# Products with v in four 64x64 pieces of TensorE, and one load of weights issued behind the next output product

## The chip, the cores and the metric

The kernel runs on one core of one Trainium2 chip. Its time is device time in microseconds. The median of the three runs shown is 1360.17 us (1358.74 to 1366.19).

TensorE is called PE here, VectorE DVE, ScalarE ACT, GpSimd POOL, SyncE SP. SP issues nearly all DMA transfers, in order, from one queue.

## The reference

An attention with a threshold is followed by a gated feed-forward block, all in float32.

```python
# q, k, v: (8, 8, 576, 64), tau: 0.02
scores = scale * np.matmul(q, k.transpose(0, 1, 3, 2))
thresh = np.max(scores, axis=-1, keepdims=True) - tau
scores = np.where(scores >= thresh, scores, -1000000000.0)
attn = np.exp(scores - np.max(scores, axis=-1, keepdims=True))
attn = attn / (np.sum(attn, axis=-1, keepdims=True) + 1e-09)
attn_out = np.matmul(attn, v)
# (batch, head, seq, dim) -> (batch * seq, head * dim) = (4608, 512)
x = attn_out.transpose(0, 2, 1, 3).reshape(4608, 512)
g = x @ w_gate                       # (512, 1536)
silu = g * (1.0 / (1.0 + np.exp(-g)))
out = (silu * (x @ w_val)) @ w_out   # (1536, 512)
```

## The kernel before, in words

**Order of the work.** Batch 0 is handled first, in a way of its own (up to about 143 us in the trace), and isn't touched. The other seven batches have four segments each, one for each pair of heads: 28 segments. A segment has three slots. In a slot PE computes the scores of three times 64 queries of two heads against all 576 keys (`slot_scores`, L1849, matmul at L1865), and DVE, ACT and POOL turn them into weights of the attention (`slot_rest`, L1870): maxima (L1886, L1888), exponential (L1911), mask with sum (L1913), scaling (L1936, L1939), transposition in blocks of 32 (L1941). A block of twelve slots belongs to one batch; `kk` counts them from 0 to 11.

In the second slot of each segment but the first (`x == 1`, so `kk` 1, 4, 7, 10) the main loop first calls `attend` for the segment before (L1946), and straight after it `slot_scores` of this slot. The last segment is attended behind the loop (L2168), where output products follow.

**The products with v.** `attend` multiplies the weights of the attention by v for two heads of 64 columns and 576 queries. The keys are spread over the 128 partitions in two halves `a` of 64 rows and, in each, nine steps `j`. Half `a` adds up in a PSUM bank of its own, `holds[a]`, over the nine steps. The innermost loop (`x`, L1960) cuts the 128 output rows (two heads of 64 columns of v) into four parts of 32: `h` is the head and `ds` the half of v's columns. So a product has 64 rows of v by 32 columns as weights, 288 columns of the attention's weights pass by it, and 2 halves by 4 parts make eight pieces of PE's array. An attend has 9 x 2 x 4 = 72 such products. In the profile a float32 product shows as two MATMUL records, each with a LDWEIGHTS record of its own: 28 x 72 x 2 = 4032 records at L1962. The scores use pieces of the same 64x32 shape (L1865, 32 products a slot).

**What fills the slots.** Between the scores of one slot and the next, PE works on the feed-forward block of the batch before: the products with w_gate and w_val in six groups `g` (`Group`, L1035, steps p1, p5, p2, p6, p3, p7, p4; matmul at L1052), then the products with w_out. Both are computed with seven products of sums in place of eight (a Strassen scheme), the latter nested once more in the batches from `DEEP` (2) on (`Deep`, L1527; matmul at L1598). How many steps stand in which slot is written out in tables (`GV`, `CD`, L2064 to L2073).

For these batches `Deep`'s steps stand in the order p1, gates_end, p2, p7, p6, p4, p5, p3 (L1547). By `CD` p1 and gates_end come in slot 9, two steps each in slots 10 and 11, p5 in slot 0 of the next block and p3 in slot 1, where it stands behind that slot's attend and scores. Two steps of the next gates, p1 and p5 of group 0, follow in the same slot 1. In the last block p5 stands ahead of the attend behind the loop, p3 behind it.

**The loads of weights.** In the batches from `DEEP` on, the weights of a group and their sums come anew from HBM, in seven parts in the ring `flow` of two places (`load_flow`, L982; DMA at L985): parts 0 to 3 (1024 KB) and parts 4 to 6 (768 KB), the "later weights". Group `g` uses place `g % 2`. `Deep` uses the same room for its sums, so the loads of the first two groups for the next batch are issued from `Deep`'s steps when the room comes free: `self.next_flow(g, part, m)` (L1838) makes a job for SP that depends on the product `m`. Group 1's later weights go where the sums for p5's product lay (`flow_end`, written from p7). p3 of group 1 reads them first; in the last batch DVE makes sums from them first (`deepen_weights`, L1195).

**What sets the order.** A planner (`Plan`, L28) walks through PE's work in the order of the program. Every job of another engine has an engine, a duration, dependencies and a rank; SP's also have a time to landing. The planner emits the jobs of each engine in the order in which they would start. So a changed dependency can change the order of the jobs in the queues of SP, DVE, ACT and POOL. PE's order is that of the program. An attend counts 4.5 us in the plan (L1965).

Of the kernel before, what the change touches and what calls it, by code (L numbers as in the profile page):

```python
# [27 lines left out]
class Plan:  # L28
# [12 lines left out]
    def job(self, eng, took, fn, *deps, rank=1, lag=0.0, moves=0.0):  # L41
        j = Job(eng, took, fn, rank, lag, moves)
        for d in deps:
            if isinstance(d, Job) and d.end is None:
                d.then.append(j)
                j.waits += 1
            elif d is not None:
                j.ready = max(j.ready, self.after(d, eng) if isinstance(d, Job) else d + self.HOP)
        if not j.waits:
            self.open[eng].append(j)  # L50
        return j
# [45 lines left out]
    def pe(self, took, fn, *deps):  # L97
        self.force(*deps)
        for d in deps:
            if d is not None:  # L100
                self.t = max(self.t, (d.end if isinstance(d, Job) else d) + self.HOP)
        self.run(self.t)
        fn()
        self.t += took
        return self.t + self.PIPE
# [39 lines left out]
def kernel(  # L145
# [11 lines left out]
    nc = tc.nc  # L157
# [6 lines left out]
    G = 32  # L164
    NG = P // G
# [3 lines left out]
    NK = NJ // 2  # L169
    SM = 512  # L170
    NT = SM // P
    SH = S // 2
# [278 lines left out]
    heads = [slice(h * D, (h + 1) * D) for h in range(2)]  # L451
# [104 lines left out]
    def attend_tile(copy=lambda xa, fn: (fn(), give_back(xa))):  # L556
        if not unattended:
            return
        if not xts:
            for u, lo in enumerate((0, 2 * XW)):  # L560
                xts["full", u] = xall[:, lo:lo + XW].rearrange("p (c n) -> p c n", c=NCC)
            xts["last", 0] = xlast
        seg, t, pT, pT2 = unattended.popleft()
        vr, vr2 = seg["v"]
        n = pT2.shape[1]
        xa = bank("xa")
        for kt in range(KT):
            for h in range(2):
                nc.tensor.matmul(xa[h * D:(h + 1) * D, 0:n], vr[:, h, kt, :], pT[:, h, kt, :],  # L569
                                 start=(kt == 0), stop=False)  # L570
        nc.tensor.matmul(xa[:, 0:n], vr2, pT2, start=False, stop=True)
        u, lo = divmod(t * P, TC)
        to = xts[("last", 0) if t == NT else ("full", u)][:, seg["i"], lo:lo + n]
        copy(xa, lambda: nc.scalar.copy(to, xa[:, 0:n]))
# [305 lines left out]
    def take(name, full=False):  # L880
        free = [b for b in banks if (not b.held if b.fixed is not None else b.n in turns)]
        if full:
            free = [b for b in free if b.full]
            return Hold(min(free, key=Bank.free_at), name) if free else None
        n = sum(b.full for b in free)
        return Hold(min(free, key=lambda b: (b.full and n == 1, max(b.free_at(), plan.t))), name)
# [17 lines left out]
    def pool_tt(out, a, b, op):  # L904
        return lambda: nc.gpsimd.tensor_tensor(out=out, in0=a, in1=b, op=op)  # L905
# [84 lines left out]
    def x_place(c, kh):  # L990
        lo = c % 2 * XW if kh == 0 else 2 * XW
        return xall[:, lo:lo + XW].rearrange("p (t c n) -> p t c n", t=2, c=2)
# [7 lines left out]
    def token_sums(c, c2, deps, eng="POOL"):  # L1000

        x11, x12, x21, x22 = (x_block(c, t, kh)[:, c2] for t in range(2) for kh in range(2))
        s1, s2, s4 = (x[:, c2] for x in xs)
        tt, took = (pool_tt, 0.75) if eng == "POOL" else (dve_tt, 0.36)
        j1 = job(eng, took, tt(s1, x21, x22, ALU.add), *deps, rank=0)
        j2 = job(eng, took, tt(s2, s1, x11, ALU.subtract), j1, rank=0)
        j4 = job(eng, took, tt(s4, x12, s2, ALU.subtract), j2, rank=0)
        j3 = job(eng, took, tt(x21, x11, x21, ALU.subtract), j1, rank=0)
        jobs = ready_x.setdefault(c, {n: [] for n in range(5)})
        for n, j in ((1, j1), (2, j2), (3, j3), (4, j4)):  # L1010
            jobs[n].append(j)
        jobs[0] += deps
# [22 lines left out]
    class Group:  # L1035
# [32 lines left out]
        def p5(self):  # L1068
            self.take_b()
            self.e = take("pe")  # L1070
            m = self.mul(self.e, self.w[2], xs[0], True, *self.w_deps[2], *ready_x[self.c][1], *self.e.deps)
            self.e.bank.full = True
            s, old = turn_of(s_bufs)
            self.s = s
            self.s5 = job("ACT", 0.55, lambda: nc.scalar.activation(s.ap, self.e.rows(), AF.Copy, scale=0.5), m, *old, rank=0)
# [38 lines left out]
        def p3(self):  # L1114
            m = self.mul(self.e, self.w[5], xs[2], False, self.s5, *self.w_deps[5], *ready_x[self.c][4])
            u = self.u1_buf
            g1 = job("DVE", 0.7, lambda: nc.vector.scalar_tensor_tensor(out=u.ap, in0=self.e.rows(), scalar=0.5, in1=u.ap, op0=ALU.mult,
                                                                        op1=ALU.add), m, self.u1, rank=0)
            self.e.read_by(g1)
            self.e.done(True)  # L1120
            self.finish(0, u, g1, self.a, self.m2)
# [405 lines left out]
    class Deep:  # L1527
# [250 lines left out]

        def p5(self):
            m = self.nested(4, self.x, False, *self.c6)  # L1780
            self.next_flow(1, 1, m)
            t, t7 = self.spaces[0:2]
            self.c5 = self.copies(t, self.x, m, *self.z)
            n, j = self.combine(t7, job("POOL", 2.2, pool_tt(t7, t7, t, ALU.add), *self.c5, *self.c7, rank=1))
            self.ship(1, 1, n, j)
            for b in u_list:
                b.jobs = [*b.jobs, j]

        def p3(self):
            m = self.nested(2, self.x, False, *self.c5)  # L1790
            n, j = self.combine(self.x, m, psum=True)
            self.done(self.x, j)
            self.ship(0, 1, n, j)
# [152 lines left out]
    def attend(seg):  # L1946
        i = seg["i"]
        b, cc = divmod(i, NP)
        base = seg["p"]
        p = pall[:, base:base + 2 * NK * SH].rearrange("p (k h j q) -> p h k j q", h=2, j=NK, q=G)  # L1950
        vr = seg["v"]
        R, rows = 2, P // 2
        holds = [take("xa") for _ in range(R)]
        assert cc < 2 or "last_product" not in state

        def fn():
            for j in range(NK):
                for a in range(R):
                    rs = slice(a * rows, (a + 1) * rows)
                    for x in range(NG):  # L1960
                        h, ds = x // 2, slice(x % 2 * G, (x % 2 + 1) * G)
                        nc.tensor.matmul(holds[a].ap()[x * G:(x + 1) * G, 0:SH].rearrange("d (i q) -> d i q", q=G),  # L1962
                                         vr[rs, h, j, ds], p[rs, h, :, j, :], start=(j == 0), stop=(j == NK - 1))

        m = pe(4.5, fn, *seg["turned"], seg["vj"], *holds[0].deps, *holds[1].deps)  # L1965
        kh, c2 = divmod(cc, 2)
        xk = x_place(b, kh)[:, :, c2, :].rearrange("p t (i a q) -> p a t i q", a=2, q=G)
        xl = xlast[:, cc, :].rearrange("p (a q) -> p a q", a=2)
        js = x_jobs.setdefault(b, [])
        lo, at_last = 0, 2 * NT * G  # L1970
        for a in range(R):
            def copy(a=a):
                nc.scalar.copy(xk[:, a], holds[a].ap()[:, lo:lo + 2 * NT * G].rearrange("p (t i q) -> p t i q", t=2, q=G))
                nc.scalar.copy(xl[:, a], holds[a].ap()[:, at_last:at_last + G])
            js.append(job("ACT", 0.65, copy, m, last_store[0] if cc == 0 else None,
                           *(sixth_kept if b == DEEP + 1 else ()), rank=0))
            holds[a].read_by(js[-1])
            holds[a].done(False)
            holds[a].bank.full = False
        if cc == NP - 1:  # L1980
            store_last(b, *js)
        if cc >= 2:
            token_sums(b, c2, js[2 * c2:2 * c2 + 2] + js[2 * cc:] + [stores[2]], "DVE" if tail[0] else "POOL")
        return m

    def store_last(b, *deps):
        w = S - SM
        last_store[0] = job("SP", 0.1, lambda: nc.sync.dma_start(out=last_hbm[:, :, b * w:(b + 1) * w], in_=xlast), *deps, lag=3.0)
# [135 lines left out]
    for s, (n, x) in enumerate((n, x) for n in range(len(halved)) for x in range(NU3)):  # L2124
        seg = halved[n]
        i, t = seg["i"], seg["tiles"][x]
# [11 lines left out]
        elif s == 1:  # L2138
            box = []
            m = pe(1.0, lambda: attend_tile(lambda *y: box.extend(y)))  # L2140
            j = job("ACT", 0.27, box[1], m, rank=0)
# [43 lines left out]
    for c in (B - 1, B):  # L2185
# [4 lines left out]
        if c < B:  # L2190
            w = SM // 2
            j = []
# [43 lines left out]
```

## Time and profile before

| | |
|---|---|
| timed runs | 1360.17, 1358.74, 1366.19 us |
| profiled execution | 1362.1 us, of which the span from first to last instruction is 1360.2 us |
| PE's clock | 0.999 of full speed |
| PE busy | 1341.3 us (99%), 15,770 matmul records |
| DVE, ACT, POOL busy | 1072.6, 876.0, 689.1 us |
| L1962, products with v | 4032 records, 129.3 us |
| L1865, scores | 5376 records in two lengths (288 and 144 columns), 165.9 us |
| L985, loads into `flow` | 84 issues, landing after 4.2 to 9.6 us, 5.0 in the median |
| queue q8, kind "instruction" | 125 packets, 2.05 MB |

The page gives busy time by engine, then the queues of the DMA, and the chain: the work that ended last, followed back to what released it. A group's line has the source line, the engine, the operation, the target and the sources, the shapes, the count, then busy time in us and the mean of one in ns, then idle time ahead of it and what ended that. A matmul's record is longer than its share of PE's time, because matmuls overlap; what counts is the time from start to start. A line of the waits has the one who waited, the one waited for, the total in us, how often, and the longest. "issue" means that the engine waited for nothing that the profile shows. A line of the timeline has the start, the length, the engine, the line, the operation and the count of the instructions drawn together in it. SPq is SP's queue of DMA issues; its lines span from the first to the last issue that were drawn together, waits between them included.

### The profile page before, as it was taken

Reading aid. Unit: us, or ns where it says so; the run is one execution under the profiler, and the core shown is the slowest. Engines: PE = TensorE matmul, PEld = TensorE weight load, DVE = VectorE, ACT = ScalarE, POOL = GpSimd, SP = SyncE. Lnnn points to the kernel's source line nnn. Section 1 sums busy time; section 2 is a strip of 40 time slices with the busy share of each in tenths; the row PEclk is TensorE's granted clock in tenths of the full one; section 3 lists DMA queues with packets and bytes.
Section 4 is the critical chain, followed back from the end, with each engine's and each line's share of the span. In section 5 each row is a group of like instructions: output and inputs, shape, how many; then the busy total and the mean of one; then the engine's idle time right before and its main releaser. Section 6 shows DMA issues by size and latency. Waiting matters only on the chain.

```text
span 1360.2 us, 39655 instructions
## 1 busy us (share of the span) xinstructions
PE 1341.3 (99%) x15770; PEld 1115.8 (82%) x15770; DVE 1072.6 (79%) x2839; ACT 876.0 (64%) x2260; POOL 689.1 (51%) x717
## 2 busy tenths in 40 slices
PE   8999999999999999999999999999999999999998
PEld 6777777787788788878887888878887789999998
DVE  6888898878887777778787877877787776787786
ACT  6888777777756767677776766776767774330330
POOL 2588397543464669624982379426952495000000
PEclk9999999999999999999999999999999999999999
DMA  8752424555525532554164515553255405424411
GB/s 196 183 187 93 81 56 134 149 137 145 152 68 162 148 98 68 152 159 127 37 188 129 150 36 147 137 151 87 89 156 145 114 22 174 158 78 147 157 61 32
DMA packets 210760, 166.28 MB, mean 122 GB/s; under 512 B 166288, under 2 KB 182160, under 8 KB 205200
## 3 DMA queue, kind: packets, MB, share of 16 engines
q1 hardware_dynamic: 206656, 162.83, 42.2%
q8 instruction: 125, 2.05, 0.6%
q10 hardware_dynamic: 3920, 0.92, 0.4%
q14 instruction: 59, 0.48, 0.1%
HBM read 141.30 MB, written 22.41 MB: 120 GB/s over the span
## 4 chain that ended last, share of the span: by engine, by line
PE 94%; DVE 2%; POOL 1%; DMA 1%; issue 1%; ACT 0%; DVEq 0%; SPq 0%; POOLq 0%
PE pb L1052 18%; PE pa L1052 12%; PE px L1598 12%; PE sc L1865 10%; PE xa L1962 9%; PE pe L1052 9%; PE po L1331 5%; PE py L1598 3%; PE pv L1256 2%; PE pg L1256 2%; PE sc L1213 2%; PE py L1607 2%; PE sc L468 1%; PE pe L1213 1%; PE tp L538 1%; PE xa L569 1%
## 5 line engine op out<-in xcount | busy, mean ns | idle before, releaser
L1913 DVE SCALAR_TENSOR_TENSOR pall<-sc,th,pall 128x288 f32<-128x288 f32 x504 | 244.4, 513 | 58.4 <-ACT pall L1911 39.9
L1052 PE MATMUL pb<-xall,big 128*128 128x256 f32 x1152 | 273.3, 380 | 0.0
L1911 ACT ACTIVATE pall<-sc,nm 128x288 f32<-128x288 f32 x504 | 232.8, 497 | 39.0 <-DVE pall L1913 38.9
L1052 PEld LDWEIGHTS pb<-xall,big 128*128 128x128 f32 x1152 | 216.5, 190 | 30.7 <-issue 2.2
L1941 DVE STREAM_TRANSPOSE pall<-pall 128x576 f32<-128x576 f32 x252 | 188.9, 764 | 30.7 <-ACT pall L1939 22.3
L1939 ACT ACTIVATE pall<-pall,ri 128x288 f32<-128x288 f32 x413 | 189.9, 528 | 30.8 <-DVE ri L1927 30.4
L1052 PE MATMUL pa<-xall,big 128*128 128x256 f32 x768 | 183.6, 382 | 0.0
L905 POOL TENSOR_TENSOR hall<-hall,tmp 128x512 f32<-128x512 f32 x80 | 102.5, 1282 | 155.3 <-DVE hall L1105 137.1
L1886 DVE TENSOR_REDUCE mx<-sc 128x2 f32<-128x576 f32 x168 | 125.7, 748 | 52.4 <-PE sc L1865 52.2
L1052 PEld LDWEIGHTS pa<-xall,big 128*128 128x128 f32 x768 | 142.9, 190 | 22.4 <-issue 2.7
L1865 PE MATMUL sc<-kT,qT 64*32 64x288 f32 (+1 forms) x5376 | 147.1, 345 | 5.0 <-issue 3.4
L1865 PEld LDWEIGHTS sc<-kT,qT 64*32 64x32 f32 x5376 | 95.9, 106 | 57.1 <-issue 18.4
L1052 PE MATMUL pe<-xall,big 128*128 128x256 f32 x576 | 137.3, 381 | 0.0
L1962 PE MATMUL xa<-pall,vall 64*32 64x288 f32 x4032 | 129.3, 404 | 0.6 <-issue 0.6
L1052 PEld LDWEIGHTS pe<-xall,big 128*128 128x128 f32 x576 | 108.4, 190 | 17.0 <-issue 2.5
L1962 PEld LDWEIGHTS xa<-pall,vall 64*32 64x32 f32 x4032 | 74.0, 107 | 48.2 <-issue 6.8
L1936 POOL TENSOR_SCALAR pall<-pall,ri 128x288 f32<-128x288 f32 x91 | 45.2, 511 | 93.3 <-DVE ri L1927 92.9
L1921 ACT COPY sums<-sums 32x6 f32<-32x6 f32 x336 | 66.6, 198 | 36.8 <-DVE pall L1913 31.9
L905 POOL TENSOR_TENSOR tmp<-tmp 128x512 f32<-128x512 f32 (+1 forms) x41 | 56.5, 1377 | 63.7 <-ACT tmp L1127 62.2
L905 POOL TENSOR_TENSOR big<-hall 128x384 f32<-128x384 f32 (+2 forms) x69 | 65.3, 970 | 33.2 <-PE pa L1052 26.1
L1104 ACT ACTIVATE vall<-tmp 128x512 f32<-128x512 f32 x96 | 60.1, 629 | 27.8 <-POOL tmp L905 13.5
L1888 DVE TENSOR_REDUCE mx<-sc 128x1 f32<-128x288 f32 x168 | 75.0, 447 | 0.0
(279 smaller groups left out, 2503.2 us busy)
## 6 DMA issues: line engine op xcount, KB each, us to landing
big<-sums_hbm SPq DMA_DIRECT2D x42, 1024.0 KB, 5.3
big<-sums_hbm SPq DMA_DIRECT2D x48, 768.0 KB, 4.4
vall<-in_v_dram SPq DMA_DIRECT2D x112, 144.0 KB, 2.9
out_dram<-big SPq DMA_DIRECT2D x32, 256.0 KB, 2.4
qT<-in_q_dram SPq DMA_DIRECT2D x112, 72.0 KB, 4.8
kT<-in_k_dram SPq DMA_DIRECT2D x112, 72.0 KB, 2.9
wo<-in_moe_w_gate_dram SPq DMA_DIRECT2D x16, 384.0 KB, 3.5
wo<-in_moe_w_val_dram SPq DMA_DIRECT2D x16, 384.0 KB, 4.1
```

Source lines behind the costliest of these rows:

```text
L905: return lambda: nc.gpsimd.tensor_tensor(out=out, in0=a, in1=b, op=op)
L1052: nc.tensor.matmul(ps[:, i], w[:, k_, i * P:(i + 1) * P], x[:, k_, :], start=first and i == k_ == 0, stop=True, skip_group_check=True)
L1331: nc.tensor.matmul(ps, h(f), w[:, f, :], start=(f == 0), stop=(f == NF2 - 1))
L1598: nc.tensor.matmul(ps, a[:, f, :], ws[n][:, f, :], start=bank_ not in begun, stop=True, skip_group_check=True)
L1865: nc.tensor.matmul(pss[h][(slice(g * G, (g + 1) * G), *part)], qT[hs, col:col + G], kT[hs, c * SH + keys[0]:c * SH + keys[1]], start=True, ...
L1886: rs.append(job("DVE", 0.72, lambda n=n, tile_=tile_: nc.vector.tensor_reduce(out=mx[:, n:n + 2, 0], in_=tile_[:, :, 0:SH], axis=AX.X, op= ...
L1888: rs.append(job("DVE", 0.42, lambda n=n, tile_=tile_: nc.vector.tensor_reduce(out=mx[:, n + 2:n + 3, 0], in_=tile_[:, :, SH:SH + SQ], axis ...
L1911: ej = job("ACT", 0.42, lambda x=x, n=n: nc.scalar.activation(ps[x], scs[x], AF.Exp, bias=nm[:, n:n + 1]), ej, masks.get((h, u - 1)), rank=0)
L1913: masks[x] = job("DVE", 0.45, lambda x=x, n=n: nc.vector.scalar_tensor_tensor(out=ps[x], in0=scs[x], scalar=th[:, n:n + 1], in1=ps[x], op0 ...
L1939: scaled.append(job("ACT", 0.46, lambda x=x, n=n: nc.scalar.activation(x, x, AF.Copy, scale=ri[:, n:n + 1]), rj, rank=rank))
L1941: seg["turned"].append(job("DVE", 0.72, lambda both=both: nc.vector.transpose(out=both, in_=both), *scaled, rank=rank))
L1962: nc.tensor.matmul(holds[a].ap()[x * G:(x + 1) * G, 0:SH].rearrange("d (i q) -> d i q", q=G), vr[rs, h, j, ds], p[rs, h, :, j, :], start=( ...
```

## The change

Two edits. In `attend` the inner loop runs over the two heads instead of over four parts of 32 columns. A product then has 64 rows by 64 columns of weights and writes 64 partitions; 9 x 2 x 2 = 36 products in place of 72, over four pieces of the array in place of eight. Operands, banks and the planned time are the same. (`heads` is `[slice(0, 64), slice(64, 128)]`, L451.)

In `Deep`, the line that issues the load of group 1's later weights for the next batch moves from p5, where it depended on p5's product, to p3, where it depends on p3's product. p5 and p3 are the last two output products of a batch. This applies to the five batches 2 to 6; `p3_flat`, used at the end of the program, isn't changed.

```diff
         def p5(self):
             m = self.nested(4, self.x, False, *self.c6)
-            self.next_flow(1, 1, m)
             t, t7 = self.spaces[0:2]
             self.c5 = self.copies(t, self.x, m, *self.z)
             n, j = self.combine(t7, job("POOL", 2.2, pool_tt(t7, t7, t, ALU.add), *self.c5, *self.c7, rank=1))
...
         def p3(self):
             m = self.nested(2, self.x, False, *self.c5)
+            self.next_flow(1, 1, m)
             n, j = self.combine(self.x, m, psum=True)
             self.done(self.x, j)
             self.ship(0, 1, n, j)
...
                     rs = slice(a * rows, (a + 1) * rows)
-                    for x in range(NG):
-                        h, ds = x // 2, slice(x % 2 * G, (x % 2 + 1) * G)
-                        nc.tensor.matmul(holds[a].ap()[x * G:(x + 1) * G, 0:SH].rearrange("d (i q) -> d i q", q=G),
-                                         vr[rs, h, j, ds], p[rs, h, :, j, :], start=(j == 0), stop=(j == NK - 1))
+                    for h, hs in enumerate(heads):
+                        nc.tensor.matmul(holds[a].ap()[hs, 0:SH].rearrange("d (i q) -> d i q", q=G),
+                                         vr[rs, h, j, :], p[rs, h, :, j, :], start=(j == 0), stop=(j == NK - 1))
```

## The prediction, made before the changed kernel ran

> **What bounds the kernel now.** I read the page's first part, then its queues and chain, then who PE waited for.
>
> ```profile
> PE 1341.3 (99%) x15770; PEld 1115.8 (82%) x15770; DVE 1072.6 (79%) x2839; ACT 876.0 (64%) x2260; POOL 689.1 (51%) x717
> ...
> q8 instruction: 125, 2.05, 0.6%
> ...
> PE 94%; DVE 2%; POOL 1%; DMA 1%; issue 1%; ACT 0%; DVEq 0%; SPq 0%; POOLq 0%
> ```
>
> ```profile
> PE sc L468 <- DVE pall L492: 3.5, 4, 1.1
> PE sc L1865 <- issue: 3.4, 5, 1.5
> PE sc L468 <- DVE cap L704: 2.0, 1, 2.0
> PE sc L1865 <- DVE pall L1913: 1.6, 1, 1.6
> PE idle L278 <- DVE pall L260: 1.3, 1, 1.3
> PE xa L1962 <- issue: 0.6, 1, 0.6
> ```
>
> PE is the bound: 99% busy, 94% of the chain. Only two of its waits lie where the change works, and both name "issue": six stops in which PE waited for no engine and no data. All others lie before 143 us, ahead of the first product with v (171.1 us). So in the loop whatever PE time is added or saved goes straight to the end.
>
> The six stops are these. I counted PE's records (LDWEIGHTS, MATMUL, semaphore) from the start. The stops come right behind records 7616, 10432, 13504, 18368, 19392 and 25536. Each is 192 above a multiple of 256. The queue q8 moved 125 packets, 2.05 MB, so 16.4 KB each; PE has 32,084 records, 257 per packet. So each packet is a block of 256 PE instructions, and PE stops where a block ends and the next hasn't come. The packets confirm it: the six late ones ended at 339.76, 451.12, 561.20, 742.84, 782.53 and 999.71 us, and PE went on 1.3 to 1.6 us after each. Beyond the normal step the stops took 0.40, 0.49, 1.62, 0.78, 0.36 and 1.30 us, together **4.95 us**. Here is the longest, in the timeline of PE and then that of SP's queue:
>
> ```profile
> 555.20 4.59 PE L1962 MATMUL xa<-pall,vall 64*32 64x288 f32 x144
> 559.59 1.65 PE L1865 MATMUL sc<-kT,qT 64*32 64x288 f32 x58
> 562.70 0.44 PE L1865 MATMUL sc<-kT,qT 64*32 64x144 f32 x6 [1.46 <-issue]
> ```
>
> ```profile
> 555.33 0.35 SPq L985 DMA_DIRECT2D big<-sums_hbm  x1
> 559.83 2.68 SPq L441 DMA_DIRECT2D vall<-in_v_dram  x4
> ```
>
> An attend followed by scores is where records go fastest: 288 (144 matmul records and their weight loads) in 4.4 us, then 128 in 1.9 us, 15 ns each. The products over 256 columns take 2 records in 215 ns. A block is asked for about 320 records before it is needed (estimate: no packet started more than 297 records ahead; the rest is the 1 us that the quickest took to start). The tightest 320 records of the loop pass in 4.4 us; from asking to usable (landing plus 1.4 us) the loop's 103 blocks took 3.5 to 9.4 us, median 4.8. Every block whose 320 records lie in an attend and its scores is therefore at risk, and PE stops if a big load stands ahead of it.
>
> **Part 1: the products with v.**
>
> ```profile
> L1962 PE MATMUL xa<-pall,vall 64*32 64x288 f32 x4032 | 129.3, 404 | 0.6 <-issue 0.6
> L474 PE MATMUL sc<-pall 64*64 64x288 f32 x32 | 4.8, 415 | 0.0
> ...
> L1962 PEld LDWEIGHTS xa<-pall,vall 64*32 64x32 f32 x4032 | 74.0, 107 | 48.2 <-issue 6.8
> L474 PEld LDWEIGHTS sc<-pall 64*64 64x64 f32 x32 | 1.9, 132 | 2.1 <-DVE pall L492 1.0 <-issue 0.3
> ```
>
> Of 4,032 records 2,016 go, and as many weight loads: 28 attends of 72 products become 28 of 36, each product being two records.
>
> *The rounds.* Record by record, an attend is 18 rounds of 8: in a round the starts are 6.7 ns apart, and the next round starts 242.5 ns after the last (288 columns). So the 8 pieces run together, and a round costs what one product costs. With four pieces it is 18 rounds of 4. The same 4.365 us, if four 64x64 pieces run together. No row shows four: L474's round has two on the diagonal, 243 ns; L569 has two beside each other on the same rows, 109 ns a round for 128 columns. Each direction overlaps; I take four together. The other end, two by two, is a rival. Weight loads get longer, 107 to 132 ns, still under 242 ns and hidden.
>
> *The entry.* The first product waits for its weights: 427 instead of 402 ns at L1962, 453 at L474. So +26 ns, 28 times: **+0.73 us**.
>
> *The exit.* 27 of 28 attends are followed by scores of the same shape, 64x32, and their first product comes 243 ns after the first of the last round, without a break. After the change the shape differs. Every change of shape in the trace has a break: 332 ns from start to start for 288 columns (242.5 without), 309 for 256 (216), 203 for 128 (109), 212 for 144 (122); it is the same when only the columns change (L569 to L571, 203) and only the rows (L474 to L569, 332). So the scores start 20 (three steps of 6.7) + 332 ns after the first of the last round, and expose 25 ns of weight load: 377 for 243, +134 ns, 27 times: **+3.62 us**. From 64x64 to 64x32 isn't in the trace; the ends are 0 (no break) and 134, and I take 134, since both kinds of change beside it have it. The Trainium skill (TensorEngine Tiling (Array Packing), Key Properties) says that changing the tiling mode, not just the tile, drains the array; by this the exit is paid, without it the sum is the second rival's.
>
> *The stops.* With 144 records in place of 288, I took every second attend record out of the trace and looked again at all stretches of 320 records: the tightest is now 8.6 us, not 4.4. Four of the 103 blocks took that long, none beside a tightest stretch. So all six stops go: **-4.95 us**. Next late would be a block of over 8.6 us in an attend.
>
> **Part 2: the load of the second group's later weights** (L985, 768 KB, five times) moves from behind the product of p5 to that of p3. Nothing is added or removed. At 555.33 us it was issued just as an attend began; the late block was asked for at about 556.2 us and started at 560.27, when the load was landing (5.0 us in the median). The stop at 1000 us is the same picture (load 993.93, block 998.78). So this edit by itself takes away the causes of 1.62 + 1.30 us, which part 1 also covers; it isn't counted twice. On SP it is moved past an output store, the load of v and the store of the last columns, which come earlier. Its new place: p3 ends at 567.9 us; SP's queue holds two output stores there until 571.5; landing takes 4.2 to 9.6 us, so 576 to 581; first read by the third product of group 1 at 590.5 us. 9 us of cover; without it PE would wait up to that excess. In the last block DVE adds up these weights (L908, four of 0.42 us at 1150.08), read by PE at 1161.25: the load would come at about 1147.8, land at 1152 to 1157 and be summed by 1159. Cost 0; at the late end DVE holds up its queue by some 2 us (what stands behind: the quarters from 1156.57), upper end +2 us.
>
> **Sum**: -4.95 + 0.73 + 3.62 = **-0.60 us**. The profiled execution took 1362.1 us (span 1360.2), so 1361.5 for such a one. The median of the timed three is 1360.17, 1.9 lower: if they stop as long, 1359.6; if what they lack is stops (3.0 us of them), 1361.5. I take the middle: **1360.5 us**.
>
> **Rivals.**
> 1. *Slower: the break isn't repaid.* Price +4.35 us, 1364.5. It decides wherever the timed runs stop for less than 4.35 us in all. For: their stops can't be seen, and 1358.74 is 3.4 below the profiled time. Against: six stops with exact places, and timed runs that spread over 7.5 us, as late blocks would make them. The Trainium skill (Runtime: NRT & Kernel Launch, Instruction fetch mechanics) describes blocks of 256 instructions, which the trace bears out, but calls the fetch mostly hidden and gives PE room for 2,048; with that room no block would be late, and this rival would hold. The trace speaks against: blocks start at most 297 records ahead. Chance 0.20.
> 2. *Faster than forecast: no break between 64x64 and 64x32.* Only the entry is paid: 1360.17 - 4.95 + 0.73 = 1356.0. Against: all changes of shape seen have one. Chance 0.12.
> 3. *The pieces run two by two*: 18 more rounds of 242.5 ns in 28 attends, +122 us, 1482. Against: L569 and L474. Chance 0.02.
> 4. *The moved load comes late* or the planner, which now places other work around it, makes an engine late in each block: over 6.8 us in all, some 1368. Chance 0.06.
> 5. *Timed runs stop longer than the profiled one* (1366.19 is 7.4 above the lowest): 8 us or more saved, 1353 or less. Chance 0.05.
> The forecast has 0.55.
>
> **The numbers.** Within 0.5% (1353.4 to 1367.0, about what a measurement of this kernel can tell from no change): the forecast, 1 and 2, less a little at the edges, 0.82; faster 0.08 (5 and the edge of 2); slower 0.10 (3, 4, the edge of 1). Range: low end rival 2, 1355.5; high end rival 1 plus 2 us for the late load, 1366.5.
>
> **What would show it.** L1962 with 2,016 records of 64x64, 4.4 us an attend; 18 rounds of 242.5 ns with 4 starts each; first product 453 ns; scores 332 ns behind the last product; no idle of PE put down to issue between 171 and 1143 us; 109 or 110 packets on q8 (15.75 blocks fewer); L985's moved load issued at the gates' first product, and no wait of PE for it. I am wrong if the scores follow without a break, if a round lasts 485 ns, if stops remain, or if PE waits for L985.

## The result, and the profile after

The changed kernel takes **1357.59 us** in the median of 11 runs (1356.68 to 1358.54); the kernel before, beside it, 1361.26 us in 11 runs (1358.04 to 1366.19). The ratio is **0.9972** (95% interval 0.9962 to 0.9983): 3.7 us faster. 1360.5 us was forecast, no change to speak of. The time lies in the range given, but the kernel became faster, clear of the interval. The profiled execution took 1357.13 us, span 1355.3.

The page after, the same lines:

```profile
PE 1343.2 (99%) x13754; PEld 1112.5 (82%) x13754; DVE 1071.6 (79%) x2839; ACT 875.8 (65%) x2260; POOL 688.9 (51%) x717
...
q8 instruction: 109, 1.79, 0.6%
...
PE 94%; DVE 2%; POOL 1%; ACT 1%; DMA 1%; issue 0%; DVEq 0%; ACTq 0%; POOLq 0%; SPq 0%
```

PE's waits after; no line names L1865 or the products with v (L1961) any more:

```profile
PE sc L468 <- DVE pall L492: 3.0, 5, 1.1
PE sc L468 <- DVE cap L704: 1.7, 1, 1.7
...
PE xa L569 <- ACT big L545: 0.3, 1, 0.3
```

PE has 2,016 records fewer and yet 1.9 us more busy time: fewer records don't make the attends shorter. What went is a wait. The two lines with "issue" at L1865 and L1962 (3.4 and 0.6 us) are gone, and 16 packets fewer came on q8. The products with v, by form, and the stretch that held the longest stop before, on PE and on SP's queue:

```profile
L1961 PE MATMUL xa<-pall,vall 64*64 64x288 f32 x2016 | 128.7, 405 | 0.0
L1961 PEld LDWEIGHTS xa<-pall,vall 64*64 64x64 f32 x2016 | 74.4, 133 | 47.3 <-issue 5.6 <-DVE pall L1913 0.3
```

```profile
552.98 4.59 PE L1961 MATMUL xa<-pall,vall 64*64 64x288 f32 x72
557.51 1.72 PE L1865 MATMUL sc<-kT,qT 64*32 64x288 f32 x64
559.15 1.60 PE L1598 MATMUL px<-wo,hall 128*128 128x128 f32 x12
```

```profile
557.61 2.73 SPq L441 DMA_DIRECT2D vall<-in_v_dram  x4
560.42 0.57 SPq L1987 DMA_DIRECT2D last_hbm<-xlast  x1
562.59 0.41 SPq L1659 DMA_DIRECT2D out_dram<-big  x1
563.04 0.46 SPq L985 DMA_DIRECT2D big<-sums_hbm  x1
```

Half the records in the same 4.59 us; the scores run through, 64 records without a hole; the load stands 10 us after the attend's start.

To compare executions I take PE's time from the start of the third slot's scores (150 to 154 us) to its last product. It is 1200.01 us in the changed kernel, where nothing stops PE, and 1202.72 in the one before. So the change itself brings **2.7 us** in the profiles. The other 2.3 us between the two spans lie ahead of that, where the change does nothing (the second slot's scores come at 141.8 us before and at 139.5 after).

### The profile page after: what moved, and what is told of

It reads as the page before. It is cut to its first block, busy times and chain, and to the rows that moved or that the text cites. A ratio compares the mean times of both kernels' runs of the same rounds, so it can differ in the third digit from the quotient of the medians.

```text
span 1355.3 us, 35619 instructions
## 1 busy us (share of the span) xinstructions
PE 1343.2 (99%) x13754; PEld 1112.5 (82%) x13754; DVE 1071.6 (79%) x2839; ACT 875.8 (65%) x2260; POOL 688.9 (51%) x717
## 4 chain that ended last, share of the span: by engine, by line
PE 94%; DVE 2%; POOL 1%; ACT 1%; DMA 1%; issue 0%; DVEq 0%; ACTq 0%; POOLq 0%; SPq 0%
PE pb L1052 19%; PE pa L1052 13%; PE px L1598 12%; PE sc L1865 10%; PE xa L1961 9%; PE pe L1052 9%; PE po L1331 5%; PE py L1598 3%; PE pg L1256 2%; PE pv L1256 2%; PE sc L1213 2%; PE py L1607 2%; PE pe L1213 1%; PE sc L468 1%; PE pv L585 1%; PE xa L569 1%
## 5 line engine op out<-in xcount | busy, mean ns | idle before, releaser
L1865 PE MATMUL sc<-kT,qT 64*32 64x288 f32 (+1 forms) x5376 | 144.9, 346 | 0.0
L1865 PEld LDWEIGHTS sc<-kT,qT 64*32 64x32 f32 x5376 | 90.9, 106 | 58.0 <-issue 25.1
L1961 PE MATMUL xa<-pall,vall 64*64 64x288 f32 x2016 | 128.7, 405 | 0.0
L1961 PEld LDWEIGHTS xa<-pall,vall 64*64 64x64 f32 x2016 | 74.4, 133 | 47.3 <-issue 5.6
```

The costliest lines, as they stand in the source:

```text
L1865: nc.tensor.matmul(pss[h][(slice(g * G, (g + 1) * G), *part)], qT[hs, col:col + G], kT[hs, c * SH + keys[0]:c * SH + keys[1]], start=True, ...
L1961: nc.tensor.matmul(holds[a].ap()[hs, 0:SH].rearrange("d (i q) -> d i q", q=G), vr[rs, h, j, :], p[rs, h, :, j, :], start=(j == 0), stop=(j ...
```

## The experiments

The theory: PE stops where its next block of 256 instructions comes late; the change takes all stops away and pays a break at 27 exits and a longer entry. Rivals: the moved load is what helps and the four pieces only cost; the difference comes from the head of the program.

**The kernel before, once more.**

> The kernel before once more, unchanged, for a second profile. Theory A (PE stops where a block of 256 instructions comes late): stops put down to issue between 171 and 1143 us, each behind a record that is 192 above a multiple of 256, at least four of them, 4 to 9 us in all with what follows them; not all in the same places, since the DMA's moments vary. Rival C (the head of the program makes a good part of the difference): the first scores of the loop start at 130.3 us and the second at 141.8 again, as in the first profile of before, and not 0.6 and 2.3 us earlier as in the changed kernel.

1360.82 us profiled. Four stops, behind records 7616, 13504, 19392 and 25536, four of the former six places, 5.2 us of gaps beyond the normal step. A fifth, behind record 10432, is too short for a line; its slot lost 0.37 us against the same slot without a stop.

```profile
PE sc L1865 <- issue: 4.5, 4, 1.7
...
PE sc L1865 <- DVE pall L1913: 1.4, 1, 1.4
```

From the third slot on it took 1202.67 us, the first profile 1202.72. Its first two slots' scores came at 128.8 and 140.1 us, 1.5 and 1.8 us earlier than in the first profile. So the head varies by itself by nearly as much as the two spans differed there, and the loss in the loop stays. The rival that the head makes the difference falls for the 2.7 us of the loop; how much of the timed 3.7 us lies in the head isn't shown.

**Part 1 alone.** The kernel before with only this edit:

```diff
-                    for x in range(NG):
-                        h, ds = x // 2, slice(x % 2 * G, (x % 2 + 1) * G)
...
+                    for h, hs in enumerate(heads):
```

> Part 1 alone: four pieces of 64x64, the load still behind p5. Theory A: half as many records in an attend are enough; no stop put down to issue between 171 and 1143 us, 27 breaks of 332 ns, time as the changed kernel's: 0.997 of before (0.996 to 0.9985). Rival B (the load at the attend's start is the cause): stops stay at some of the five attends behind p5, 0.5 to 2 us each, and the time is 0.998 to 1.000.

1357.64 us against 1359.76, ratio 0.9982 (0.9974 to 0.9991). No stop in the loop; 1200.06 us from the third slot on, as with both edits. The load is issued right after the attend's start, as before, and nothing comes late:

```profile
553.90 4.59 PE L1961 MATMUL xa<-pall,vall 64*64 64x288 f32 x72
558.42 1.72 PE L1865 MATMUL sc<-kT,qT 64*32 64x288 f32 x64
```

```profile
554.03 0.40 SPq L985 DMA_DIRECT2D big<-sums_hbm  x1
```

So half the records are enough, and in the loop the moved load adds nothing to them. Fewer records also put the blocks' ends elsewhere, and four pieces with other ends weren't run. But five of the six late blocks of the first profile were usable 5.4 to 6.4 us after they were asked for (the sixth 9.4), and with four pieces no 320 records of the loop pass in under 8.6 us, wherever a block ends.

**Part 2 alone.** The line moved from p5 to p3, eight pieces of 64x32 kept.

> Part 2 alone: eight pieces of 64x32, the load moved behind p3. Theory A: the stops at the attends behind p5 go (3.3 of 6.5 us in the first profile), those at other attends stay, no breaks: 0.9975 (0.9965 to 0.9985), as good as the change as a whole. Rival B: nearly all stops go and 1353 to 1355 us are reached (0.995), since no breaks are paid. If the load is no cause: 1.000 and stops behind p5 as before.

1356.14 us against 1359.76, 0.9971 (0.9961 to 0.9982): by itself it does as much as the whole change. The stops behind p5 are gone (560 and 1000 us), and with the other timing that at 743 us as well; three are left:

```profile
PE sc L1865 <- issue: 1.0, 3, 0.5
```

From the third slot on 1198.39 us, 1.6 less than with four pieces: it keeps 1.5 us of gaps and pays no breaks.

**More transfers at the attends**, in the kernel before and in the changed one. Nothing reads the copy:

```diff
+            was = halved[n - 1]
+            job("SP", 0.1, lambda lo=was["p"]: nc.sync.dma_start(out=spare_hbm, in_=pall[:, lo:lo + 6 * SH]), *was["turned"], plan.t,
+                lag=2.0, moves=3.4)
             prepare_v(seg, attend(halved[n - 1]))
```

> The kernel before with one more transfer at each of 27 attends: 884 KB of the attention's weights copied to a spare place in HBM (nothing reads it), issued by SP when these weights are ready and the attend is planned. Theory A: with full transfers in the way the block comes late at most attends where one ends; some 10 or more stops, 10 to 25 us more in all, 1.007 to 1.02. Rival (stops depend on the place in the program alone and not on transfers): 1.000 to 1.002.

> The changed kernel with the same extra copy of 884 KB at 27 attends that made the kernel before 1.2% slower (10 stops, 15 us). Theory A: with half the records the delay still fits; none or two short stops, 0.997 to 1.000 of before, at most 3 us above the changed kernel. Rival (the copies cost time by something else than stops, such as late operands): 1.007 to 1.012 here too.

Before: 1376.16 us against 1359.76, 1.0122 (1.0097 to 1.0147). Ten stops, 15.7 us of gaps beyond the normal step, each at the end of a block, up to 3.4 us:

```profile
PE sc L1866 <- issue: 12.8, 8, 3.3
...
PE xa L1963 <- issue: 1.4, 2, 1.0
```

The longest, where two big transfers stand one behind the other ahead of the block:

```profile
563.16 1.65 PE L1866 MATMUL sc<-kT,qT 64*32 64x288 f32 x59
568.07 0.69 PE L1866 MATMUL sc<-kT,qT 64*32 64x144 f32 x5 [3.26 <-issue]
```

```profile
558.90 0.47 SPq L986 DMA_DIRECT2D big<-sums_hbm  x1
559.49 0.37 SPq L2131 DMA_DIRECT2D spare_hbm<-pall  x1
```

The changed kernel with the same copies: 1357.43 us against 1361.72, 0.9970 (0.9959 to 0.9982), no stop, 1200.01 us. So by themselves the transfers cost nothing, and half the records stand them.

In the kernel before, the ten stops cost more than their gaps: against slots without a stop 24.7 us. At the three longest (2.7, 3.4 and 3.2 us) the trace shows a granted clock of 0.5 for 3.4, 6.8 and 3.4 us, and their slots lost 1.9, 3.1 and 1.9 us beyond the gap; the other seven, of up to 2.2 us, left the clock at 1.0 and lost 0.2 to 0.5 us beyond it.

**Half a block further on.** In the kernel before, 128 short records at the head, while PE waits for its first data:

```diff
+    short = bank("idle")
+    for _ in range(32):
+        nc.tensor.matmul(short[0:G, 0:G], ones[0:G, 0:G], ones[0:G, 0:G], start=True, stop=True)
+    give_back(short)
```

> The kernel before with 32 short idle products (32x32 weights, 32 columns; 128 records of PE, about 2 us while PE waits for the first loads) at the head, whose result nothing reads. All later instructions lie half a block further on. Theory A (the block's end decides): stops again only behind records that are 192 above a multiple of 256, so at other places of the program: none of the places of before (340, 452, 560, 743, 783, 1000 us); instead some of those where 320 records now pass in under 5 us (near 240, 306, 376, 488, 526, 596, 635, 705, 742, 962, 1032, 1070 us), most likely 705 and 742, where a load of weights stands ahead of the attend. Two to six stops, 1 to 7 us; 0.997 to 1.002. Rival (the places are set by the transfers or by the program's steps alone): stops again near 340, 560, 783 and 1000 us.

1356.70 us against 1361.26, 0.9962 (0.9945 to 0.9980). Three stops, behind records 6848, 17600 and 27584, each 192 above a multiple of 256: near 305, 704 and 1070 us, three of the twelve places named, none of the old ones. A fourth, behind record 15552 at 633 us, also on the list (635), is too short for a line; its slot lost 0.27 us. Of the two called most likely, 705 us came and 742 did not. The ratio lies a little under the range expected, 0.997 to 1.002.

```profile
702.72 1.40 PE L1869 MATMUL sc<-kT,qT 64*32 64x288 f32 x37
705.10 0.71 PE L1869 MATMUL sc<-kT,qT 64*32 64x144 f32 x27 [0.97 <-issue]
```

```profile
698.47 0.35 SPq L989 DMA_DIRECT2D big<-sums_hbm  x1
```

32 idle products make the kernel before about as fast as the change did: from the third slot on it took 1200.04 us. The end of the block decides where PE stops.

**Holding back the other loads.** To the load behind p3, this adds: the loads that were issued just before an attend wait in a list until its scores are in the program.

```diff
+                if self.g == 1 and not tail[0]:
+                    held.append((load_flow, (self.c, self.g + 2, 0)))
+                else:
+                    load_flow(self.c, self.g + 2, 0, plan.t + plan.PIPE)
...
+                elif self.g == 3 and not tail[0]:
+                    held.append((load_flow, (self.c, self.g + 2, 1, m)))
...
         pss, mark = slot_scores(seg, t)
+        if x == 1:
+            release(mark)
```

(`release` issues the jobs in the list, with the end of the scores as a further dependency in the plan; `load_sums` of group 3 in batch 1 is held in the same way.) First with eight pieces of 64x32, then with four of 64x64:

> The kernel before with the load behind p3 and, besides, the other loads of weights that were issued just before an attend held back until its scores are planned (group 3's first parts, group 5's later parts, and in batch 1 group 3's sums); eight pieces of 64x32. Theory A: the three stops that part 2 alone left (1.5 us of gaps, 2.0 with what follows them) go, none or one stop stays, no breaks are paid: 0.9955 of before (0.9945 to 0.9965), some 2 us under part 2 alone and 3.5 to 4 under the changed kernel. Rival (stops only move to other attends): as part 2 alone, 0.997.

> The same held loads with four pieces of 64x64. With no stops on either side the difference to the run before it is what the shape costs by itself. Theory A: 27 exits and 28 entries at 0.15 us, +4.1 us: 0.9985 of before, as the changed kernel. If the breaks are hidden somewhere: as the run before it.

Eight pieces: **1353.92 us** against 1361.72, 0.9949 (0.9935 to 0.9962), the best version here. One stop is left (338 us):

```profile
PE sc L1880 <- issue: 0.5, 1, 0.5
```

Four pieces, same loads: 1357.66 us, 0.9975 (0.9965 to 0.9985), no stop, 1200.01 us from the third slot on against 1196.94. The one stop made its slot 0.86 us longer than the same slot without one. With that taken off, eight pieces need 1196.1: four pieces cost 3.9 us. That is the shape by itself.

## Why the prediction was wrong

The mechanism was right in its main parts: PE stops at late blocks, half the records take the stops away, and every change of shape costs a break. Two of its sizes and one choice were off: the stops went into the sum with 4.95 us and cost 6.6, the breaks with 4.35 and cost 3.9, and the timed runs were taken to stop less than the profiled one.

- **The stops.** Place, cause and disappearance were right. Their size wasn't: I counted the gaps, 4.95 us. Slot by slot against runs without them (the kernel with both edits for three, part 2 alone for the others), the six cost 0.64, 0.71, 1.85, 1.25, 0.60 and 1.53 us, together **6.6 us**. Behind a gap the records of the first round are longer (307 ns for 282; the 25 ns are what an exposed weight load costs at an attend's start, 427 for 402), and the rounds of eight come broken. Together that is 0.2 us for five of them and 0.5 us for the one inside an attend. The prediction's four blocks of 8.6 us or more leave one out: the late block of 742.84 us took 9.4 us, over 320 records that passed in 8.4. Its stop, too, is gone in the changed kernel.
- **The breaks.** 332 ns at each of the 27 exits and 453 ns at the entries, as worked out; four pieces run together, rounds of 242.5 ns with starts 6.7 ns apart (the first round of an attend 293 ns, for 266 before). From the scores ahead of an attend to those behind it PE took 0.137 us longer, and in the next slot 0.014, together 0.151 instead of 0.161: the exposed weight load of the scores' first product shows as 14 ns, not 25. At the first attend the next slot gave the loss back. So the breaks cost **3.9 us**, not 4.35.
- **The sum** would then have been -6.6 + 3.9 = -2.7 us, as measured, in place of -0.6. A small difference of two terms that are each seven or eight times as large moves by as much as their errors.
- **From the profile to the timed runs.** I took the profile's 1.9 us above the median of three runs as a hint that timed runs stop less, and moved the forecast up from 1359.6 to 1360.5. The runs speak against it: what they gain, plus 3.9 us of breaks, is 7.6 us in this comparison, and 6.0 to 8.2 us in the other three with a kernel whose profile shows no stop. So they lose about as much as the profile's 6.6 us, or more; how much of it lies in stops can't be seen in them. The spread points the same way: 8.2 us before, 1.9 us after. Part of it goes with the clock: of 45 runs of the kernel before beside the experiments, the 14 with a granted clock of 1.0 took 1359.1 us in the mean and the seven with 0.997 or less 1363.5. Whether the clock fell behind stops there, as it did with the added copies, isn't shown; the version with held loads and four pieces, without a stop in its profile, also has one such run (0.997, 1360.68 us).
- **Part 2** costs nothing, as said: no wait of PE for it. It was issued at 563.0 us, during p3 and not behind it: the data it overwrites are p5's, so only the planner's order holds it, not p3's end. In the last blocks DVE waits 5.4 us for the loads of L985 instead of 3.2, and PE doesn't notice.
- **Rival 1** (the break isn't repaid, 1364.5) falls: taking the stops away brings 6.6 us, 1.7 times what the breaks cost. The Trainium skill (Runtime: NRT & Kernel Launch, Instruction fetch mechanics) calls the fetch of instructions mostly hidden. Where PE's records go at 15 ns each it isn't, with 6.6 us here. **Rival 2** (no break from 64x64 to 64x32) falls with 332 ns at all 27. The Trainium skill (TensorEngine Tiling (Array Packing), Key Properties) says that a change of tiling mode drains the array, and these breaks agree with it. **Rival 3** falls with the rounds of 242.5 ns, **rival 4** since no wait of PE names L985 or another engine in the loop. **Rival 5** falls in its size: 3.7 us were saved and not 8.

Where the timed runs stop, and for how long, stays open: only profiled executions show it.

## What to carry to other kernels

Where PE waits for "issue", count its records and look whether the waits stand a multiple of 256 apart (here each 192 above one); then look for the densest stretch of about 320 records and the big transfers issued just ahead of it. Moving the transfers cost nothing here; halving the records held against all transfers tried, but a change of shape costs its break each time. And size a stop by the same stretch of a run without it, not by the gap alone.

## What the runs showed of the hardware

- A block of 256 PE instructions comes later when large transfers stand ahead of it: ten stops, and up to 3.4 us, with a copy of 884 KB at 27 attends, six and up to 1.6 us without. In the changed kernel a block was usable 3.3 to 11.8 us after it was asked for (both ends estimated as in the prediction) and none was late: the tightest 320 records took 8.6 us, the slowest block had 18.7 us, and the least time to spare was 2.7 us.
- In all three stops of 2.7 us or more the granted clock fell to 0.5, late in the stop or within 0.6 us behind it, for 3.4 or 6.8 us. It stayed at 1.0 in all shorter ones (up to 2.2 us).
- Without stops the loop repeats to 0.05 us: 1200.01, 1200.06, 1200.01 and 1200.01 us from the third slot on, in four kernels with four pieces and different transfers.
